# One load moved back in SyncE's queue, and a decoding list started three steps later

## The chip, the cores and the metric

One core of a Trainium2 chip runs the kernel. The metric is device time in microseconds (us), the median of the runs.

## The reference

Three layers in a row. First a linear attention over 2 x 8 heads, 768 positions and 48 channels, with a decay per channel and a bonus for the current position. Its output is read as 1536 tokens of 384 channels. Then a mixture of eight experts:

```python
expert_idx = np.argmax(x @ w_gate, axis=1)
# token i goes to row counts[e] of its expert e while counts[e] < capacity
h = np.maximum(np.einsum('ecd,edf->ecf', disp, w1), 0.0)
y = np.einsum('ecf,efd->ecd', h, w2)
out[i] = gate_w[i] * y[expert_idx[i], pos[i]]
```

with 1024 hidden channels for each expert. Last a gated MLP, `(sigmoid(x @ w_gate) * (x @ w_val)) @ w_out`, with 1536 hidden channels. All in float32.

## The kernel before, in words

Everything is written for one core in an order given by hand; each engine carries out its instructions in that order, and only waits for the data and the buffers of each.

The attention stage ends with the router: it ranks the tokens of each expert, and twelve indirect DMAs from GpSimd (`scatter`, L221) write the scaled tokens to a table in DRAM, `xs_d`, with a stretch of rows for each expert. Expert zero's tokens are also gathered on TensorE, so that its work can begin before the last scatters land.

The expert stage is one loop (L940) of 64 steps, eight for each expert, step i = 8e + f, and three more that finish. A step holds:

- `s1(e, f)` (L891): nine matmuls of 224 columns, the first product for 128 hidden channels. Numbers are split in a high and a low float32r part, hence three matmuls for each of three slices. The relu goes out of PSUM through ScalarE (L903, high part) and VectorE (L904, low part). There are three PSUM buffers `ph`.
- `s2` of step i - 3 (L910): six matmuls, the second product. In steps 7 to 9 and at the experts' borders a list shifts some of them.
- `etr(e, b)` (L876): the transposes of one half b of an expert's rows on TensorE (L883), then `xh` by ScalarE (L886) and `xl` by VectorE (L887). Both halves use the one PSUM tile `xp`. Expert one's two halves stand in step 7, each ahead of one `s2`; for later experts they are in steps f = 4 and f = 6 of the expert before.
- `eload(e)` (L872): the load of an expert's rows from `xs_d`, on SyncE's queue. It waits for all twelve scatters. Expert e + 2's is in step f = 5 of expert e; expert one's stands ahead of the loop (L936).
- `bg` (L135): it converts one expert weight block, a 384 KB tile `raw`, to its high part `rh` on ScalarE (L144) and its low part `rl` on VectorE (L146). Ahead of that it calls `fetch` (L128), which issues the loads of blocks up to five ahead on SyncE. Blocks 0 to 4 are converted in the attention stage; step i converts block 5 + i and, from step 1 on, issues the load of block 9 + i. (Block n is called raw n for short.) Block n uses the buffer of block n - 5 (`NRAW` = 5), so its load waits for the conversion of that one. Blocks 2k and 2k + 1 hold the first and second weights of steps 2k and 2k + 1.
- `tick` (L206): it takes the next operation of a list, `dops`. The list holds the decoding of five blocks of the MLP's weights, 768 KB each as 64-bit numbers: a load on SyncE (`dfetch`, L156, two buffers) and seven operations: one on ScalarE (L166), four on VectorE (L169, L172, L176, L180), the high part on ScalarE (L186) and the low part on GpSimd (L190). Five loads and 35 operations make 40 entries. The first two entries are loads. `tick(2)` ahead of the loop takes them; after that one entry goes with each step from step `T0` to 39, and two with each from step 40.

So SyncE's queue ahead of the loop is: blocks 5 to 9, expert one's rows, two MLP blocks; then blocks 10 to 13 (steps 1 to 4), expert two's rows (step 5), block 14, and so on.

After the expert stage the MLP stage runs 48 steps of matmuls (L1001, L1026) and scatters the output.

Of the kernel before, what the change touches and what calls it, by code (L numbers as in the profile page):

```python
# [21 lines left out]
AHEAD = 5  # L22
OVL = 6
FIRST = 5
T0 = 6
TK = 1
RS = {(5, 1): (0, 1), (6, 0): (2, 3, 4, 5)}
R4E = "ssvsvs"
# [21 lines left out]
NT = 2  # L50
TAILF = 2
EB0 = 7
S20 = {7: (4, 5), 8: (6,), 9: (7,), 10: ()}
EB = (4, 6)
DMAX = (122880.0 - 2.0 ** -7) * 2.0 ** 16
# [54 lines left out]
def body(tc, A, out):  # L110
    nc = tc.nc
    E = mybir.EngineType
    with ExitStack() as top, tc.manual_schedule():
# [14 lines left out]
        def fetch(n):  # L128
            while nxt[0] < n:
                m = nxt[0]  # L130
                nxt[0] += 1
                raw[m] = rpl[0].tile([128, 768], F32, tag="raw", name="raw", bufs=rpl[1])
                nc.sync.dma_start(out=raw[m], in_=A["wx"][m // 2][:, (m % 2) * 768:(m % 2) * 768 + 768])

        def bg(count=1, pool=False, ahead=3, later=None):  # L135
            for _ in range(count):
                n = nxt[1]
                if n == 64:
                    return
                nxt[1] += 1  # L140
                fetch(min(n + ahead, rpl[2]))
                t = raw.pop(n)
                h = rh[n % NR]
                nc.scalar.copy(out=h, in_=t)  # L144
                if later is None:
                    (nc.gpsimd if pool else nc.vector).tensor_sub(rl[n % NR], t, h.bitcast(F32))  # L146
                else:
                    later.append(lambda l=rl[n % NR], t=t, h=h: nc.vector.tensor_sub(l, t, h.bitcast(F32)))
# [57 lines left out]
        def tick(count=1, keep=False):  # L206
            last = None
            for _ in range(count):
                if dops:
                    n, k, f = dops.pop(0)  # L210
                    if keep and (k == 5 and last == n or k == 6 and kept):
                        kept.append(f)
                    else:
                        f()
                    if k == 4:
                        last = n
# [12 lines left out]
        def after(load, done):  # L229
            for i in done:  # L230
                tc.add_manual_dep(load.ins, i.name,
                                  mybir.DependencyInfo(mybir.DependencyClass.Sync, mybir.DependencyReason.DATA),
                                  reason="rows of every scatter")
# [541 lines left out]
        with ExitStack() as ctx:  # L775
# [7 lines left out]
            def c1():  # L783
                ct = pm.tile([128, 8], F32, tag="xp", name="ct", bufs=1)
                nc.tensor.matmul(ct, ones, cnts[:, 0, :], start=True, stop=False)
                nc.tensor.matmul(ct, ones, cnts[:, 1, :], start=False, stop=True)
                nc.vector.tensor_copy(out=cf, in_=ct)
                nc.vector.memset(off[:, 0:1], 0.0)
                for e in range(7):
                    nc.vector.tensor_add(off[:, e + 1:e + 2], off[:, e:e + 1], cf[:, e:e + 1])  # L790
                nc.vector.tensor_copy(out=offi, in_=off[0:1, :])
                nc.vector.reduce_max(out=mxi, in_=cf[0:1, :], axis=AX.X)
# [67 lines left out]
            def c2(b):  # L860
                x, m2, oh, rank, pi, gk = R[b][0:6]
                t = rt.tile([128, 6, 8], F32, tag="tm", name="tm2")
                nc.vector.tensor_mul(t, oh, off.unsqueeze(1).to_broadcast([128, 6, 8]))
                s = rt.tile([128, 6], F32, tag="se", name="se2")
                nc.vector.reduce_sum(out=s, in_=t, axis=AX.X)
                nc.vector.tensor_add(cpos[:, 6 * b:6 * b + 6], s, rank)

            def c3(e):
                offv[e] = nc.values_load(offi[0:1, e:e + 1], engines=[E.DVE, E.Activation], min_val=0, max_val=1536,
                                         skip_runtime_bounds_check_because="expert counts sum to the number of tokens")  # L870

            def eload(e, eng=nc.sync):  # L872
                xr[e] = mp.tile([128, 2, 384], F32, tag="xr", name="xr")
                after(eng.dma_start(out=xr[e][0:NP], in_=xs_d[e * 1536:e * 1536 + NB, :].rearrange("(b p) d -> p b d", p=NP)), scx)

            def etr(e, b):  # L876
                r = xr[e]
                if b == 0:
                    xt[e] = (mp.tile([128, 3, NB], F32R, tag="xh", name="xh", bufs=1),
                             mp.tile([128, 3, NB], F32R, tag="xl", name="xl", bufs=1)) if e % 2 else (xeh, xel)  # L880
                xp = pm.tile([128, 3, NP], F32, tag="xp", name="xp", bufs=1)
                for kt in range(3):
                    nc.tensor.transpose(xp[:, kt, :], r[0:NP, b, kt * 128:(kt + 1) * 128], ident[0:NP, 0:NP])  # L883
                q = slice(b * NP, b * NP + NP)
                xh, xl = xt[e]
                nc.scalar.copy(out=xh[:, :, q], in_=xp)  # L886
                nc.vector.tensor_sub(xl[:, :, q], xp, xh[:, :, q].bitcast(F32))  # L887
# [3 lines left out]
            def s1(e, f):  # L891
                n = 8 * e + 2 * (f // 2)
                wh, wl = rh[n % NR], rl[n % NR]
                xh, xl = xt[e]
                ph = pm.tile([128, NB], F32, tag="ph", name="ph", bufs=3)
                mm = [(kt, a, b) for kt in range(3) for a, b in ((wh, xh), (wh, xl), (wl, xh))]
                if e == f == 0:
                    mm = mm[0::3] + mm[2::3] + mm[1::3]
                for i, (kt, a, b) in enumerate(mm):
                    w = slice(((f % 2) * 3 + kt) * 128, ((f % 2) * 3 + kt) * 128 + 128)  # L900
                    nc.tensor.matmul(ph, a[:, w], b[:, kt, :], start=(i == 0), stop=(i == 8))  # L901
                h = hp.tile([128, 2, NB], F32R, tag="hh", name="hh")
                nc.scalar.activation(out=h[:, 0, :], in_=ph, func=AF.Relu)  # L903
                nc.vector.scalar_tensor_tensor(out=h[:, 1, :], in0=ph, scalar=0.0, in1=h[:, 0, :].bitcast(F32), op0=ALU.max,  # L904
                                               op1=ALU.subtract)
                hs[(e, f)] = h
# [26 lines left out]
            xt[0] = (xeh, xel)  # L933
            plan(PRE)
            fetch(sum(BG) + FIRST)
            eload(1)  # L936
            tick(2)
            seq = [(e, f) for e in range(8) for f in range(8)]
            LAG = 3
            for i in range(64 + LAG):  # L940
                if i == OVP:
                    overflow()
                if i < 64:
                    e, f = seq[i]
                    s1(e, f)
                    if i == 3:
                        c2(0)
                        c2(1)
                    if i == 1:
                        c1()  # L950
                    if i == OVL:
                        offv["most"] = nc.values_load(mxi[0:1, 0:1], min_val=0, max_val=1536,
                                                      skip_runtime_bounds_check_because="at most every token")
                    if f == 3 and e:
                        c3(e)
                    if f in EB and 0 < e < 7:
                        etr(e + 1, EB.index(f))
                    if f == 5 and e < 6:
                        eload(e + 2)
                if i >= LAG:  # L960
                    e, f = seq[i - LAG]
                    if i < 66 - TAILF:
                        for g in (() if f == 0 and e else (0, 1) if f == 1 and e else S20.get(i, (f,))):
                            if i == EB0:
                                etr(1, g - S20[i][0])
                            s2(e, g)
                        if (f == 7 if i > max(S20) else i == max(S20) - 1):
                            for m in range(3):
                                yev(e, m)
                    elif i == 66:  # L970
                        for m in range(3):
                            for g in range(7 - TAILF, 8):
                                s2(7, g, (m,))
                            yev(7, m)
                            xsplit(0, m)
                if sum(BG) - 5 <= i <= 58 and i != OVP - 1:
                    bg(2 if i == OVP else 1, False, AHEAD)
                if i < 64:
                    tick(0 if i < T0 or OVP - NT <= i < OVP else TK if i < 40 else 2)
            tick(len(dops))  # L980
# [97 lines left out]
```

## Time and profile before

| | us |
|---|---|
| median of 3 runs | 463.74 |
| lowest and highest | 463.63, 464.53 |
| the profiled execution | 464.22 |
| its span | 462.5 |
| TensorE busy (PE) | 441.7 (96%) |
| weight loads (PEld) | 415.8 (90%) |
| VectorE (DVE) | 281.8 (61%) |
| ScalarE (ACT) | 218.2 (47%) |
| GpSimd (POOL) | 111.2 (24%) |

The profile is of one execution. The span is from its first to its last instruction; 1.7 us of the execution's own time lie around it. Busy time is that of each engine's instructions; SyncE only issues DMAs. The expert stage lies between 84.4 us and 225 us, the MLP stage after it. PEclk is the clock that TensorE was granted, as a share of 2.4 GHz; 0.5 is the level of 1.2 GHz.

### The profile page before, as it was taken

How to read it: one execution, taken by the hardware profiler on the slowest of the kernel's cores; microseconds unless marked ns; L12 is line 12 of the kernel's file. 1: busy time of each engine (PE TensorE's matmuls, PEld its weight loads, DVE VectorE, ACT ScalarE, POOL GpSimd, SP SyncE). 2: the span in 40 equal slices, each digit the busy share in tenths (PEclk: the TensorE clock that was granted, in tenths of full speed). 3: DMA queues.
4: the chain of work that ended last, by engine and by line, in shares of the span. 5: the costliest groups of instructions: out<-in, count | busy, mean ns of one | idle time of the engine just before them, and what ended most of it. 6: DMA issues, size and time to landing. Idle time of an engine off the chain costs nothing.

```text
span 462.5 us, 8319 instructions
## 1 busy us (share of the span) xinstructions
PE 441.7 (96%) x3227; PEld 415.8 (90%) x3230; DVE 281.8 (61%) x502; ACT 218.2 (47%) x469; POOL 111.2 (24%) x105
## 2 busy tenths in 40 slices
PE   8999999956999999999999999999999999999994
PEld 4688887946999999999889999999999999999993
DVE  6867876736999999775477878777442222222211
ACT  3377778505777776674444343444343222212222
POOL 2555475700202112000033544313113000000013
PEclk9999999996999999999999999999999999999999
DMA  7999904676789876773024353422002000000002
GB/s 242 338 300 320 373 19 141 236 270 217 225 257 302 273 229 203 221 219 142 0 69 122 85 135 71 136 85 54 2 17 87 0 1 1 0 1 0 1 10 92
DMA packets 23194, 63.53 MB, mean 137 GB/s; under 512 B 4592, under 2 KB 8304, under 8 KB 23152
## 3 DMA queue, kind: packets, MB, share of 16 engines
q1 hardware_dynamic: 21088, 58.24, 40.7%
q0 software_dynamic: 1920, 4.73, 2.8%
q8 instruction: 26, 0.43, 0.4%
q14 instruction: 16, 0.13, 0.1%
q10 hardware_dynamic: 144, 0.00, 0.0%
HBM read 55.48 MB, written 7.48 MB: 136 GB/s over the span
## 4 chain that ended last, share of the span: by engine, by line
PE 45%; DVE 3%; issue 2%; ACT 1%; POOL 1%; POOLq 0%; DVEq 0%; ACTq 0%
PE po L1026 15%; PE pv L1001 14%; PE pg L1001 14%; PE ph L901 1%; PE py L920 1%; POOL out_dram L221 1%; DVE wa L176 1%; DVE wa L169 1%; DVE gl L1013 1%; DVE sg L1011 0%; PE py L919 0%; ACT wa L166 0%; ACT x0h L930 0%; DVE wa L172 0%; ACT wy L186 0%
## 5 line engine op out<-in xcount | busy, mean ns | idle before, releaser
L1011 DVE TENSOR_TENSOR sg<-sg,pv 128x384 f32<-128x384 f32 (+2 forms) x49 | 26.6, 543 | 80.5 <-PE pv L1001 79.6
L146 DVE TENSOR_TENSOR rl<-raw,rh 128x768 fp32r<-128x768 f32 x59 | 60.4, 1024 | 19.7 <-ACT rh L144 19.3
L144 ACT CAST rh<-raw 128x768 fp32r<-128x768 f32 x64 | 53.1, 833 | 24.6 <-DMA raw<-in_wx_dram 12.0
L920 PE MATMUL py<-hh,rh 128*128 128x448 f32 x192 | 64.3, 377 | 0.0
L1012 ACT CAST gh<-sg 128x384 fp32r<-128x384 f32 (+2 forms) x49 | 24.8, 506 | 81.9 <-DVE sg L1011 80.5
L190 POOL TENSOR_TENSOR wy<-wa,wy 128x768 fp32r<-128x768 f32 x10 | 20.2, 2023 | 146.5 <-ACT wy L186 116.1
L1013 DVE TENSOR_TENSOR gl<-sg,gh 128x384 fp32r<-128x384 f32 (+2 forms) x49 | 35.8, 730 | 29.4 <-ACT gh L1012 27.9
L919 PE MATMUL py<-hh,rl 128*128 128x224 f32 x192 | 53.1, 276 | 0.0
L1007 ACT ACTIVATE sg<-pg 128x384 f32<-128x384 f32 x48 | 23.5, 490 | 56.9 <-PE pg L1001 56.0
L221 POOL DMA_INDIRECT out_dram<-ob,ids x12 | 11.7, 974 | 119.5 <-ACT ob L1033 117.0
L920 PEld LDWEIGHTS py<-hh,rh 128*128 128x128 f32 x192 | 36.8, 192 | 2.0
L919 PEld LDWEIGHTS py<-hh,rl 128*128 128x128 f32 x192 | 37.3, 194 | 0.0
L1026 PE MATMUL po<-wy,gh 128*128 128x384 f32 x144 | 36.7, 335 | 0.0
L903 ACT ACTIVATE hh<-ph 128x224 fp32r<-128x224 f32 x64 | 22.9, 357 | 24.7 <-PE ph L901 23.5
L372 ACT ACTIVATE at<-cst,dl 128x128 f32<-128x128 f32 x84 | 26.1, 391 | 10.1 <-DVE dl L358 10.1
L904 DVE SCALAR_TENSOR_TENSOR hh<-ph,hh 128x224 fp32r<-128x224 f32 x64 | 24.6, 384 | 10.0 <-ACT hh L903 9.0
L901 PE MATMUL ph<-xh,rh 128*128 128x224 f32 x96 | 26.6, 277 | 0.3 <-PEq L795 0.3
L901 PE MATMUL ph<-xh,rl 128*128 128x224 f32 x96 | 26.8, 280 | 0.0
L901 PE MATMUL ph<-xl,rh 128*128 128x224 f32 x96 | 26.7, 278 | 0.0
L901 PE MATMUL ph<-xeh,rh 128*128 128x224 f32 x96 | 26.2, 275 | 0.0
L901 PE MATMUL ph<-xeh,rl 128*128 128x224 f32 x96 | 26.1, 275 | 0.0
L1026 PEld LDWEIGHTS po<-wy,gh 128*128 128x128 f32 x144 | 26.0, 188 | 0.0
(208 smaller groups left out, 1195.4 us busy)
## 6 DMA issues: line engine op xcount, KB each, us to landing
raw<-in_wx_dram SPq DMA_DIRECT2D x64, 384.0 KB, 5.2
r<-in_wy_dram SPq DMA_DIRECT2D x18, 768.0 KB, 5.8
dm<-in_dm_dram SPq DMA_DIRECT2D x8, 672.0 KB, 11.6
kt<-in_kr_dram SPq DMA_DIRECT2D x8, 576.0 KB, 11.3
xs_d<-zero SPq DMA_DIRECT2D x8, 336.0 KB, 10.0
xr<-xs_d SPq DMA_DIRECT2D x8, 336.0 KB, 7.0
v<-in_v_dram SPq DMA_DIRECT2D x8, 288.0 KB, 8.9
cat<-in_cax_dram SPq DMA_DIRECT2D x1, 404.0 KB
```

The costliest lines, as they stand in the source:

```text
L144: nc.scalar.copy(out=h, in_=t)
L146: (nc.gpsimd if pool else nc.vector).tensor_sub(rl[n % NR], t, h.bitcast(F32))
L372: nc.scalar.mul(AT[s][:, j, :], ident, DL[s][:, j:j + 1])
L901: nc.tensor.matmul(ph, a[:, w], b[:, kt, :], start=(i == 0), stop=(i == 8))
L904: nc.vector.scalar_tensor_tensor(out=h[:, 1, :], in0=ph, scalar=0.0, in1=h[:, 0, :].bitcast(F32), op0=ALU.max, op1=ALU.subtract)
L919: nc.tensor.matmul(y[:, 0, :], wl[:, w], h[:, 0, :], start=(f == 0), stop=False, skip_group_check=True)
L920: nc.tensor.matmul(y, wh[:, w], h, start=False, stop=(f == 7), skip_group_check=True)
L1001: nc.tensor.matmul(pg[g], w[a][:, q], x[b][:, kt, :], start=(kt == 0 and (a, b) == (0, 0)), stop=(kt == 2 and b == 1))
L1011: nc.vector.tensor_mul(gg[:, a:b], sg[:, a:b], pg[1][:, a:b])
L1012: nc.scalar.copy(out=gh[:, a:b], in_=gg[:, a:b])
L1013: nc.vector.tensor_sub(gl[:, a:b], gg[:, a:b], gh[:, a:b].bitcast(F32))
L1026: nc.tensor.matmul(po[i], g[v][:, a], w[u][:, q], start=(f == 0 and (u, v) == (0, 0)), stop=(f == 11 and v == 1))
```

## The change

The load of expert one's rows moves from ahead of the loop to the end of step 3, behind that step's `bg`, and one `tick` goes with it instead of two ahead of the loop. `T0` goes from 6 to 9.

```diff
-T0 = 6
+T0 = 9
...
+LOAD1 = 3
...
             fetch(sum(BG) + FIRST)
-            eload(1)
-            tick(2)
             seq = [(e, f) for e in range(8) for f in range(8)]
...
                     bg(2 if i == OVP else 1, False, AHEAD)
+                if i == LOAD1:
+                    eload(1)
+                    tick()
                 if i < 64:
                     tick(0 if i < T0 or OVP - NT <= i < OVP else TK if i < 40 else 2)
```

SyncE's queue is then: blocks 5 to 9; blocks 10, 11 and 12 (steps 1 to 3); expert one's rows and one MLP block; block 13 (step 4); expert two's rows and block 14 (step 5); and so on. The second MLP block's load goes with step 9, the first decoding operation with step 10, and the list ends in step 43 instead of 41.

## Rows read from the trace of the kernel before

**Rows 1.** Stretches: window, length, busy and count per engine, PEclk, DMA share, GB/s.

```profile
88.00:92.00 4.00, 4.00 (x33) 3.91 (x33) 3.64 (x16) 2.59 (x6) 3.39 (x3) 1.00 0.32 111
92.00:96.00 4.00, 4.00 (x34) 3.92 (x33) 3.86 (x12) 1.19 (x2) 0.08 (x1) 1.00 0.33 99
96.00:100.00 4.00, 2.36 (x18) 1.86 (x16) 0.14 (x1) 0.00 (x0) 0.00 (x0) 1.00 0.91 307
100.00:104.00 4.00, 0.00 (x0) 0.00 (x0) 0.00 (x0) 0.00 (x0) 0.00 (x0) 0.79 0.96 366
...
108.00:112.00 4.00, 3.86 (x16) 3.73 (x17) 2.02 (x4) 1.17 (x2) 0.00 (x0) 0.50 0.66 204
...
140.00:160.00 20.00, 20.00 (x158) 19.57 (x157) 18.91 (x30) 15.15 (x29) 3.25 (x2) 1.00 0.90 277
```

**Rows 2.** Waits of the span: engine, line, waited for, us in total, times, longest.

```profile
ACT rh L144 <- DMA raw<-in_wx_dram: 12.0, 3, 10.9
...
PE xp L883 <- DVE xl L887: 9.4, 1, 9.4
```

**Rows 3.** Timeline of TensorE, 94 to 118 us: start, us, instruction, idle before.

```profile
95.74 0.26 PE L901 MATMUL ph<-xeh,rh 128*128 128x224 f32 x1
...
97.28 0.51 PE L883 MATMUL xp<-cst,xr 112*128 112x112 f32 x3 [0.38 <-DMA xr<-xs_d]
...
98.37 0.38 PE L920 MATMUL py<-hh,rh 128*128 128x448 f32 x1
108.14 0.82 PE L883 MATMUL xp<-cst,xr 112*128 112x112 f32 x3 [9.39 <-DVE xl L887]
...
110.54 0.39 PE L901 MATMUL ph<-xh,rh 128*128 128x224 f32 x1
...
112.43 0.36 PE L919 MATMUL py<-hh,rl 128*128 128x224 f32 x1
```

**Rows 4.** Timeline of VectorE, 94 to 124 us.

```profile
95.76 0.38 DVE L904 SCALAR_TENSOR_TENSOR hh<-ph,hh 128x224 fp32r<-128x224 f32 x1
105.15 0.96 DVE L146 TENSOR_TENSOR rl<-raw,rh 128x768 fp32r<-128x768 f32 x1 [9.01 <-ACT rh L144]
...
107.57 0.51 DVE L887 TENSOR_TENSOR xl<-xp,xh 128x336 fp32r<-128x336 f32 x1
109.47 0.51 DVE L887 TENSOR_TENSOR xl<-xp,xh 128x336 fp32r<-128x336 f32 x1 [1.38 <-ACT xh L886]
```

**Rows 5.** Timeline of ScalarE, 94 to 124 us.

```profile
104.28 0.83 ACT L144 CAST rh<-raw 128x768 fp32r<-128x768 f32 x1 [10.88 <-DMA raw<-in_wx_dram]
```

**Rows 6.** Timeline of SyncE's queue, 50 to 145 us.

```profile
94.01 0.33 SPq L874 DMA_DIRECT2D xr<-xs_d  x1
94.93 0.81 SPq L158 DMA_DIRECT2D r<-in_wy_dram  x2
95.85 3.23 SPq L133 DMA_DIRECT2D raw<-in_wx_dram  x4
99.13 0.43 SPq L874 DMA_DIRECT2D xr<-xs_d  x1
```

**Rows 7.** Timeline of GpSimd, 66 to 94 us, the last scatter.

```profile
90.50 1.58 POOL L221 DMA_INDIRECT xs_d<-xs,pi  x1 [0.30 <-DVE mxi L792]
```

**Rows 8.** Timeline of VectorE, 66 to 94 us, the low parts of blocks 5 and 7.

```profile
87.09 0.96 DVE L146 TENSOR_TENSOR rl<-raw,rh 128x768 fp32r<-128x768 f32 x1 [0.33 <-issue]
...
91.44 0.95 DVE L146 TENSOR_TENSOR rl<-raw,rh 128x768 fp32r<-128x768 f32 x1
```

**Rows 9.** Views of lines L133 (weight blocks) and L874 (experts' rows): landing times.

```profile
DMA to landing us min/median/max: 3.1/5.2/14.4
...
DMA to landing us min/median/max: 7.0/7.6/8.2
```

**Rows 10.** Timeline of VectorE, 168 to 196 us.

```profile
180.19 0.96 DVE L180 SCALAR_TENSOR_TENSOR wa<-r,wa 128x768 int32<-128x768 int32 x1
181.07 0.39 DVE L904 SCALAR_TENSOR_TENSOR hh<-ph,hh 128x224 fp32r<-128x224 f32 x1
```

## The prediction, on record before the change was run

> **What bounds the kernel now.** I read the span in stretches first, then the waits, then each engine's timeline around the one hole, then SyncE's queue. The stretches [rows 1] show TensorE busy for all of 88 to 96 us and again from 112 us on (20.00 of 20.00 us in 140 to 160), while 96 to 100 holds 2.36 us of work and 100 to 104 none. The clock is granted in full at first; the share for 100 to 104 is 0.79 and for 108 to 112 it is 0.50, so TensorE, idle since 98.7, falls to the 1.2 GHz level and restarts there.
>
> The waits name the hole [rows 2]: one wait of 9.4 us of a transpose of expert one's rows (L883) for VectorE's xl, and on ScalarE a longest wait of 10.9 us for a weight load. The timelines join them. TensorE [rows 3] does the first half's transposes of expert one (97.28, step 7), six matmuls of step 4's second product up to 98.4, and then the second half's transposes only at 108.14, because both halves share one PSUM tile, which VectorE must empty. VectorE [rows 4] has nothing to do from 95.76 + 0.38 to 105.15, then two subtractions and two relu halves, and only then xl at 107.57. The first subtraction waits for ScalarE's conversion of weight block raw 10, which started at 104.28 after 10.88 us of idling for that load [rows 5]. So one late load, at the head of two in-order engines, holds TensorE, which does not need that block before step 10.
>
> Why it is late stands in SyncE's queue [rows 6]: the load of expert one's rows goes out at 94.01, two 768 KB loads of MLP blocks from 94.93, and raw 10 to 13 only from 95.85. The first of them waited for the scatters, the last of which GpSimd issued from 90.50 to 92.08 [rows 7]. Raw 10 itself needs just the buffer of raw 5, which VectorE was done with at 87.09 + 0.96 = 88.05 [rows 8]. In 88 to 92 the DMA share was 0.32 [rows 1]: there was room.
>
> **The change, part by part.** *The load moves behind raw 10, 11 and 12.* These three no longer wait for the scatters. Raw 10 goes out at about 88.1 instead of 95.85, and raw 12 when raw 7's subtraction ends, 91.44 + 0.95 = 92.4 [rows 8]; raw 11 lies between, about 91.3. A raw load lands 3.1 to 14.4 us after issue, median 5.2 [rows 9]; with nothing but one another and the scatters ahead I take the median. Raw 10 is then there at 93.3, before ScalarE and VectorE come to it. Raw 11 lands at about 96.5 and its conversion ends 0.83 later [rows 5], at 97.3, just when VectorE wants it (below): no slack, and every microsecond more is paid in full. The bounds are no cost (3.1 us) and 9.2 us (14.4 us).
>
> *The load of expert one's rows itself* still waits for the scatters, so it goes out at 94.01 at the earliest. Now it lands after 97.28 - 94.01 = 3.27 us [rows 3, 6]; the other loads of this line need 7.0 to 8.2 us [rows 9], each behind an MLP block and a weight block just issued. Here raw 11 and 12 went out 2.7 and 1.6 us before it; 384 KB take 1.1 us at the 366 GB/s of 100 to 104 [rows 1], so little is left of them. I take 0.4 us over today: rows at 97.7, bounds 97.3 and 102.6 (8.2 us after 94.4).
>
> The DMA page of the Trainium skill (DMA: Bandwidth & Descriptors, section Queues, rings and completion order) has a rule against this: each DMA engine takes its queue rows in turn, packet by packet, so raw 11 and 12 would halve the pace of the last scatters, which now run alone. No run here shows it yet; by that rule the rows would come some 0.7 us later than today, and the time would be about 0.3 us above my sum.
>
> *The chain to the end of step 8's first product.* VectorE: after the relu half of 95.76 the next subtraction can start at about 96.1; from there to xl it needs what it needs now, 107.57 - 105.15 = 2.42 us [rows 4], so xl ends at 96.1 + 2.42 + 0.51 = 99.0. TensorE: from transposes to the end of xl the second half takes 109.47 + 0.51 - 108.14 = 1.84 us, with transposes of 0.82 us at the 1.2 GHz level; at 2.4 GHz they take 0.51 [rows 3], so 1.53. Rows at 97.7 give xl at 99.2, the later of the two. The second half follows 0.06 us on, its xl ends at 100.8, and step 4's and 5's second products run beside this. Step 8's nine matmuls need that xl from the second one on; at 0.12 us each (33 or 34 in 4 us, [rows 1]) they end at 101.8. Now they run from 110.54 to 112.43, at half the clock [rows 3]. The gain is 112.43 - 101.8 = **10.6 us**, the clock included. Were TensorE to wait for nothing after the rows arrive at 97.3, step 8 would end at about 97.3 + 2 x 0.3 (transposes) + 12 x 0.16 + 1.06 = 100.9: 11.5 us is the most.
>
> *What is late next.* Raw 13 goes out behind the rows (336 KB) and now one MLP block instead of two, at about 95.4. Raw 10, behind both, took from 95.85 to 104.28 at most, 8.4 us [rows 5, 6]; so raw 13 lands by 103.8. Behind it on ScalarE stands the relu of step 9; TensorE first misses that when step 12 wants its PSUM buffer, about 106.6, which leaves raw 13 until 105.0. I cost it at nothing. Expert two's rows follow raw 13 and are wanted at step 12 as well.
>
> *Decoding from step nine.* The second MLP block's load moves to step 9's tick, and ScalarE's first decoding op from step 6 to step 10. Of the 40 operations in the list, one goes behind the moved load, 31 in steps 9 to 39, and 8 in steps 40 to 43 at two a step; now it is 34 in steps 6 to 39 and the last 4 in steps 40 and 41. No operation is added. What it takes out of steps 6 to 9 also leaves ScalarE free in front of xh: with the start kept at step 6 that operation would wait there for the MLP block. In the end four more double ticks lie on VectorE. Today the last two decoding operations of step 40 end at 180.19 + 0.96, and step 41's relu half starts at 181.07 [rows 10], ends at 181.46, and is wanted when step 44 reuses its buffer, about 182.2: 0.7 us to spare. After the change the two fall in step 42, with step 40 free of them, so I take nothing, with bounds of 0 and 1.9 us (both operations uncovered).
>
> *The rest.* From step 9 to the end TensorE is busy throughout [rows 1], with the same work, so the gain should reach the end undiminished. **Sum:** the profiled execution took 464.22 us (span 462.5 and 1.7 around it), 464.22 - 10.6 = 453.6. The median of the runs is 463.74, 0.48 lower, so on that footing 453.1.
>
> **The rivals.** *A, the loads come late* (chance 0.14): the rows land as the six others of this line did, 7.6 us after issue, at 102.0, or raw 11 does. TensorE then idles for over 5 us and falls to 1.2 GHz as now, which costs about 2 us of restart (half of 108.14 to 112.43): gain 10.6 - 4.3 - 2 = 4.3, time 459.4; half as late and without the clock, 455.2. For it: six of seven loads of this line are that slow. Against: what stands ahead of them.
>
> *B, VectorE becomes the bound* (0.10): decoding now meets each expert's transposes (xl, twice 0.5 us) instead of its output additions, and the end is denser. Price 1 to 3 us, 454.1 to 456.1. For it: 0.7 us of slack today. Against: no long wait of TensorE for VectorE appears after 112 us, and VectorE starts with four operations fewer.
>
> *C, no change* (0.02): the load order doesn't matter because the DMA engines limit, the hole just moving to raw 13: 463.7. Against: the share of 0.32 in 88 to 92.
>
> *D, slower* (0.03): the wait moves to the rows. The first half's transposes stand in front of everything on TensorE, where the late weight block of today stood behind six matmuls. If the rows land later than 97.7 + 10.6 - 2, about 106.3 (the clock then falls too), the time passes today's; at the 14.4 us of the longest raw load, from 94.4, they land at 108.8: some 2.5 us above, 466.2. Against: 12 us are half as much again as the worst landing of this kind.
>
> **How the numbers follow.** My forecast (gain 10 to 11.5, 452.2 to 453.8) has 0.71, the likeliest single value being 453.1. The range reaches down to the most that the chain can give, 463.74 - 11.5 = 452.2, and up to 455.6, which takes in most of B and the milder half of A; about 0.13 stays outside. A measurement here tells about 0.2 per cent, 0.93 us, from no change. Faster: forecast, A and B, 0.95; same 0.02; slower 0.03.
>
> **What would show it.** In the profile after: raw loads on SyncE at about 88, 91 and 92, before the rows at 94 to 95; ScalarE's 10.9 us wait gone; the second transposes of expert one near 99 instead of 108.14; the clock at full from 96 to 116; TensorE's work from step 9 on unchanged and about 10.6 us earlier. Wrong would be a wait of over 1 us for the rows (A, D), new waits of L901 or L883 for VectorE near steps 40 to 46 (B), or ScalarE waiting for raw 13 beyond step 12 (C).

## The result, and the profile of the changed kernel

The changed kernel takes 455.82 us (median of 4 runs, 455.30 to 456.54) against 463.84 us of the kernel before beside it (4 runs, 463.63 to 464.53): a ratio of 0.9826, 95% interval 0.9806 to 0.9845. It is 8.0 us faster, and the forecast was 10.6 us and 453.1 us; 455.8 lies 0.2 us above the range. The profiled execution took 456.54 us, its span 454.8. All lines of the code have moved down by one (L883 is L884, L919 is L920).

One thing is needed for the runs that follow: in some executions of several kernels the attention stage ends about 1 to 5 us later (step 0 begins at 85 to 90 us instead of 84), in code that no kernel here changes; so I read times before step 9 only in profiles in which step 0 begins near 84 us, and name the others.

TensorE's timeline of the changed kernel, 98 to 112 us, answers to [rows 3]: the transposes of expert one's two halves, the matmul that follows step 8's first product, and expert two's transposes.

```profile
99.28 0.51 PE L884 MATMUL xp<-cst,xr 112*128 112x112 f32 x3 [2.40 <-DMA xr<-xs_d]
...
100.86 0.74 PE L884 MATMUL xp<-cst,xr 112*128 112x112 f32 x3
...
104.76 0.28 PE L920 MATMUL py<-hh,rl 128*128 128x224 f32 x1
...
110.67 0.46 PE L884 MATMUL xp<-cst,xr 112*128 112x112 f32 x3
```

The 9.4 us wait for `xl` is gone and the second transposes stand at 100.86 instead of 108.14. In its place stands a wait of 2.40 us for the rows themselves. Step 8's first product ends at 104.76, where it ended at 112.43 before: 7.67 us, and the spans differ by 7.7 us, so all that was won by then reached the end. The forecast had that point at 101.8.

SyncE's queue, which answers to [rows 6]:

```profile
78.35 14.37 SPq L134 DMA_DIRECT2D raw<-in_wx_dram  x8
95.76 0.33 SPq L875 DMA_DIRECT2D xr<-xs_d  x1
96.15 0.45 SPq L159 DMA_DIRECT2D r<-in_wy_dram  x1
96.70 0.37 SPq L134 DMA_DIRECT2D raw<-in_wx_dram  x1
```

The eight weight loads (raw 5 to 12) are all out by 92.4 to 92.7, as forecast, and ScalarE no longer waits for one. But the rows leave at 95.76 instead of 94.01, though GpSimd issues the last scatter at the same time as before:

```profile
90.47 1.58 POOL L222 DMA_INDIRECT xs_d<-xs,pi  x1 [0.30 <-DVE mxi L793]
```

VectorE's timeline, 94 to 104 us, answers to [rows 4]:

```profile
98.07 0.38 DVE L905 SCALAR_TENSOR_TENSOR hh<-ph,hh 128x224 fp32r<-128x224 f32 x1
100.30 0.51 DVE L888 TENSOR_TENSOR xl<-xp,xh 128x336 fp32r<-128x336 f32 x1 [1.85 <-ACT xh L887]
102.11 0.51 DVE L888 TENSOR_TENSOR xl<-xp,xh 128x336 fp32r<-128x336 f32 x1 [1.30 <-ACT xh L887]
```

VectorE is ready at 98.45 and idles for the rows: the engine that was the cause is not late any more. The stretches (the columns of [rows 1]) show what the wait costs:

```profile
96.00:100.00 4.00, 1.60 (x14) 1.41 (x14) 2.45 (x5) 1.29 (x3) 0.00 (x0) 1.00 0.82 268
100.00:104.00 4.00, 3.89 (x18) 3.46 (x17) 1.97 (x3) 1.43 (x3) 0.00 (x0) 0.62 1.03 336
104.00:108.00 4.00, 4.00 (x31) 3.92 (x30) 2.03 (x4) 2.15 (x6) 0.00 (x0) 0.95 0.67 259
```

In 100 to 104 TensorE is busy for 3.89 us but ends 18 instructions where 33 go in 4 us of full clock: the granted clock is 0.62 on average there. Behind the idle 2.40 us TensorE went down to 1.2 GHz once more: read microsecond by microsecond, the clock is 0.50 from 101 to 104 and 1.00 again from 105.

The DMA engines show what holds the rows. One microsecond, 89 to 90 us, of the kernel before (first) and of the changed one (second), queue by queue: packets, MB, share of 16 engines. Queue q0 carries the scatters, q1 what SyncE issues.

```profile
q0 software_dynamic: 44, 0.18, 50.5%
```

```profile
q1 hardware_dynamic: 34, 0.10, 90.1%
```

Before, 44 packets of the scatters move 0.18 MB. After, raw 10 begins here: 34 packets of 3 KB hold 90.1% of the engines (14.4 engine-us over 34 packets, 0.42 us each; in 84 to 85 us of the kernel before, where weight loads move alone, 152 packets of 2.7 KB hold 103.0% for the same time, 0.11 us each), and not one packet of a scatter moves. Much the same comes again in 92 to 93 us, as raw 11 begins.

```profile
q1 hardware_dynamic: 20, 0.06, 88.1%
q0 software_dynamic: 10, 0.02, 6.1%
```

### The profile page after: what moved, and what is told of

It reads as the page before. It is cut to its first block, busy times and chain, and to the rows that moved or that the text cites. A ratio compares the mean times of both kernels' runs of the same rounds, so it can differ in the third digit from the quotient of the medians.

```text
span 454.8 us, 8312 instructions
## 1 busy us (share of the span) xinstructions
PE 440.9 (97%) x3227; PEld 415.3 (91%) x3230; DVE 282.0 (62%) x502; ACT 218.1 (48%) x469; POOL 109.9 (24%) x105
## 4 chain that ended last, share of the span: by engine, by line
PE 46%; DVE 3%; issue 2%; ACT 1%; POOL 1%; POOLq 0%; DVEq 0%; ACTq 0%
PE po L1028 15%; PE pv L1003 15%; PE pg L1003 15%; PE ph L902 1%; PE py L921 1%; POOL out_dram L222 1%; DVE wa L177 1%; DVE wa L170 1%; DVE gl L1015 1%; DVE sg L1013 0%; PE py L920 0%; ACT wa L167 0%; ACT x0h L931 0%; DVE wa L173 0%; ACT wy L187 0%
## 5 line engine op out<-in xcount | busy, mean ns | idle before, releaser
L920 PE MATMUL py<-hh,rl 128*128 128x224 f32 x192 | 53.0, 276 | 0.0
L191 POOL TENSOR_TENSOR wy<-wa,wy 128x768 fp32r<-128x768 f32 x10 | 18.7, 1872 | 140.3 <-ACT wy L187 140.3
L920 PEld LDWEIGHTS py<-hh,rl 128*128 128x128 f32 x192 | 37.2, 194 | 0.0
L373 ACT ACTIVATE at<-cst,dl 128x128 f32<-128x128 f32 x84 | 26.1, 392 | 10.6 <-DVE dl L359 10.6
L902 PE MATMUL ph<-xh,rl 128*128 128x224 f32 x96 | 26.7, 278 | 0.0
L902 PE MATMUL ph<-xh,rh 128*128 128x224 f32 x96 | 26.4, 275 | 0.3 <-PEq L796 0.3
L902 PE MATMUL ph<-xl,rh 128*128 128x224 f32 x96 | 26.6, 277 | 0.0
L902 PE MATMUL ph<-xeh,rh 128*128 128x224 f32 x96 | 26.2, 275 | 0.0
L902 PE MATMUL ph<-xeh,rl 128*128 128x224 f32 x96 | 26.1, 275 | 0.0
```

The lines of the kernel that those rows point to most:

```text
L373: nc.scalar.mul(AT[s][:, j, :], ident, DL[s][:, j:j + 1])
L920: nc.tensor.matmul(y[:, 0, :], wl[:, w], h[:, 0, :], start=(f == 0), stop=False, skip_group_check=True)
```

## The experiments

Two theories on the late rows. **S**: the weight loads take from the scatters by their bytes, so fewer bytes ahead bring the rows back to 94. **P**: each weight load that starts beside the scatters holds them 1 to 1.5 us, whatever its size. A third, **T**, says that the start of the decoding and not the load's place decides the time. Kernels of one paragraph ran on one chip.

**The two parts alone, half the bytes, the products first.** The first of these keeps `T0` = 6 and moves the load, the second does the reverse:

```diff
-T0 = 9
+T0 = 6
```

> The moved load alone; decoding starts at step 6 again (its second MLP block goes out with step 6, its first operation comes with step 7). Theory S (the last scatters share the DMA engines with raw 10 to 12, so expert one's rows leave and land about 2 us later than before, and TensorE's clock falls): the start of decoding is not what was won or lost; rows again leave at about 95.7 and land near 99.3, time 455.3 to 456.6, as with the whole change. Rival D (the later start of decoding carries a part of the gain, since its first operation stood ahead of xh on ScalarE): 457 or more, with a new wait of ScalarE or VectorE in 100 to 110 us.

> Decoding from step 9 alone; the load of the rows and the two MLP blocks stay ahead of the loop. Theory S: the late raw 10 stays, TensorE still waits some 9.4 us for xl, time 463.0 to 464.5. Rival D: faster than 462.5.

The load alone: 459.25 us (456.18 to 462.57, 7 runs), 0.9913 [0.9874, 0.9952]. The later decoding alone: 465.10 us (8 runs), 1.0032 [1.0016, 1.0048]. T falls: the load carries the gain. But the profile of the first (456.18 us, span 454.4) holds a second lesson. Its rows leave at 95.31 and its clock stays up, so step 8's first product ends at 102.82, 1.94 us ahead of the changed kernel, and its span is only 0.4 us shorter. What it loses again lies far behind. The stretch of 160 to 180 us of this kernel, and its one long wait there:

```profile
160.00:180.00 20.00, 19.25 (x152) 18.62 (x151) 18.35 (x31) 14.11 (x27) 5.71 (x3) 1.00 0.64 191
```

```profile
PE py L920 <- DVE x L926: 0.7, 1, 0.7
```

The changed kernel works 20.00 us in the same stretch and has no such wait; here TensorE waits 0.7 us for an addition of an expert's output on VectorE (L926). From expert two's first transposes to the end this kernel needs 345.67 us; the changed kernel needs 454.8 - 110.67 = 344.13, the kernel before 462.5 - 118.43 = 344.07. The other half of the change needs 345.85, and in its 180 to 200 us TensorE works 18.62 of 20 us, with a wait of 1.38 us for VectorE ahead of an expert's transposes (190.43). The first decoding operation stands in step 6 before, in 7 in the first of these kernels, in 9 in the second, in 10 in the changed one. So it seems to matter where the list's operations fall on the eight steps of an expert: of the four starts, 7 and 9 cost 1.5 to 1.8 us more than 6 and 10. That it is this phase is argued from four kernels, not varied further, and the two waits shown are half of the loss in the first and most of it in the second.

The third loads only the first half of raw 10 to 12; it leaves the second half out, and the conversions read the first half twice (that part of the edit isn't shown):

```diff
+HALF = (10, 11, 12)
...
-                nc.sync.dma_start(out=raw[m], in_=A["wx"][m // 2][:, (m % 2) * 768:(m % 2) * 768 + 768])
+                c = 384 if m in HALF else 768
+                nc.sync.dma_start(out=raw[m][:, 0:c], in_=A["wx"][m // 2][:, (m % 2) * 768:(m % 2) * 768 + c])
...
```

> The changed kernel, but raw 10 to 12 load only half of their bytes (192 KB each; the conversions read that half twice, so the weights of these three blocks are not the reference's and the engines' work is the same). Theory S: half the competing bytes, so about half of the 1.75 us go: rows leave at 94.6 to 95.1, land near 98.2, the clock falls for a shorter time or not at all, time 453.9 to 455.2. Rival Q (the rows leave late for a reason that has nothing to do with the bytes ahead, such as their place in SyncE's queue or a late write receipt): rows leave at 95.6 to 95.9, time 455.3 to 456.6.

It took 455.03 us (453.58 to 459.27), 0.9826 [0.9761, 0.9892], but in its profile step 0 begins at 86.1 us and raw 12's place in the queue holds the rows, not the scatters (rows out at 96.41). It tells nothing on S and P, and was run again below. The fourth changes step 7: the second products of steps 4 to 7 there, the halves of the transposes behind the second and third of them.

```diff
-S20 = {7: (4, 5), 8: (6,), 9: (7,), 10: ()}
+S20 = {7: (4, 5, 6, 7), 8: (), 9: (), 10: ()}
...
-                            if i == EB0:
-                                etr(1, g - S20[i][0])
                             s2(e, g)
+                            if i == EB0 and g in (5, 6):
+                                etr(1, g - 5)
```

> The changed kernel, but in step 7 the second products of steps 4 and 5 stand ahead of the first transposes of expert one's rows, that of step 6 between the halves and that of step 7 behind the second half (they were in steps 7, 7, 8 and 9). Theory S (the miss is TensorE idling for late rows, then running at 1.2 GHz): twelve matmuls fill 1.9 of the 2.4 us, the clock stays at 2.4 GHz or falls for under 1 us, the gap left is 0.5 to 1 us at the rows and 0.2 to 0.5 at step 8; time 452.2 to 453.5. Rival (the conversions on VectorE, not the rows, set step 8's start): 454.5 or more, with TensorE waiting for xl.

458.41 us (452.95 to 458.96, 4 runs), 0.9849 [0.9785, 0.9913]. The profile has step 0 at 89.43 us, so it shows only that the products cover the wait for the rows (0.20 us left of it) when these come late; inconclusive as to time.

**The changed kernel again; the rows first; raw 12 behind the rows.** The last of these ran with step 7 as it is, and with the products first.

```diff
             fetch(sum(BG) + FIRST)
+            eload(1)
...
-                    eload(1)
                     tick()
```

```diff
-LOAD1 = 3
+LOAD1 = 2
```

> The changed kernel once more, for comparison on this chip. Theory S (the last scatters share the DMA engines with raw 10 to 12): where step 0 starts at about 84.4 us the rows leave near 95.7 and land near 99.3, time 455.3 to 456.6. Where the attention stage ends late by x us, the rows are held by raw 12, which waits for step 2's conversion, and the time is longer by up to x, since no stall is left to swallow x: up to 460 for x of 5. Rival (the spread has nothing to do with the end of the attention stage): spans counted from step 0 differ by more than 1.5 us.

> Expert one's rows stay ahead of the loop as before the change, so they wait for the scatters in front of raw 10; only the two MLP blocks move (the first to step 3, the second to step 9). Theory S: rows leave at 94.0 and land at 97.3, raw 10 leaves at 94.4 and lands at 98 to 99 instead of 104.3, so most of the gain comes without moving the rows; TensorE's second transposes at 102 to 103, idle for some 4 us, clock falls, time 455.5 to 457.5. Rival (raw 10 has to leave before the scatters are through for any of the gain): 460 or more.

> The load of the rows one step earlier, behind raw 10 and 11 alone; raw 12 follows the rows and the first MLP block. Theory S: less traffic beside the last scatters, rows leave at 94.3 to 95.2 and land at 97.8 to 98.6, raw 12 still in time for step 7's conversion; 0.5 to 1.5 us faster than the changed kernel in the same call. Rival Q (the rows' lateness does not depend on raw 12's bytes): within 0.4 us of the changed kernel, or slower because raw 12 comes late.

> As the last one, and in step 7 the second products of steps 4 and 5 ahead of the first transposes, those of steps 6 and 7 behind the first and the second half. Theory S: TensorE has work through the wait, the clock stays at 2.4 GHz in 96 to 108 us, 2 to 4 us faster than the changed kernel in the same call, 452 to 453.5 where step 0 starts at 84.4 us. Rival (VectorE's conversions set step 8's start): within 1 us of the changed kernel.

The changed kernel: 457.77 us (454.64 to 460.70, 5 runs), 0.9852 [0.9790, 0.9914]. In its profile step 0 begins at 89.62 us, and from expert two's transposes to the end it needs 458.0 - 113.81 = 344.19 us, no more than before: what is longer lies ahead of them. With the rows ahead of raw 10 and only the MLP blocks moved: 459.25 us (7 runs), 0.9876 [0.9835, 0.9917]. Its rows leave at 93.99, with the scatters as undisturbed as before, but raw 10 to 12 only go out from 94.82, and the old wait is back at half its length:

```profile
103.22 0.82 PE L884 MATMUL xp<-cst,xr 112*128 112x112 f32 x3 [4.51 <-DVE xl L888]
```

So taking two 768 KB loads from ahead of raw 10 is worth about half of the gain (4.1 of the 7.7 us by which the spans differ), and the load's place the rest. With `LOAD1` = 2: 457.48 us (456.66 to 459.53), 0.9880 [0.9836, 0.9924], and with the products first 456.36 us (453.58 to 458.52), 0.9844 [0.9790, 0.9899]; neither can be told from the changed kernel. The profile of `LOAD1` = 2 has step 0 at 84.28, and its rows leave at 96.01 though raw 12 isn't ahead of them: raw 12's bytes don't hold them. That leaves raw 10 and 11, which both start among the scatters. The line below shows the wait for the rows, 2.60 us, and transposes that take 0.82 us, as at the low clock of [rows 3], not 0.51.

```profile
99.37 0.82 PE L884 MATMUL xp<-cst,xr 112*128 112x112 f32 x3 [2.60 <-DMA xr<-xs_d]
```

**The rows behind raw 10 alone; half the bytes again; two loads each.** The first moves `eload(1)` to step 1 and leaves the tick; the third splits each of raw 10 and 11 into two DMAs.

```diff
+                if i == 1:
+                    eload(1)
                 if i == LOAD1:
-                    eload(1)
                     tick()
```

```diff
-                nc.sync.dma_start(out=raw[m], ...
+                for c in ((0, 384), (384, 768)) if m in (10, 11) else ((0, 768),):
+                    nc.sync.dma_start(out=raw[m][:, c[0]:c[1]], ...
```

> Load of expert one's rows right behind raw 10 alone, at step 1 of the expert loop; raw 11 and 12 go out after it, the tick of the MLP's decoding stays where the change has it. Theory P (each weight load that starts beside the scatters holds their packets for 1 to 1.5 us, whatever its size): one start instead of two lies ahead of the rows, so they go out about 0.8 to 1.2 us earlier than in the changed kernel, at 94.5 to 95.0 us where step 0 starts at 84.3, and the clock stays up, since TensorE's wait falls under 2 us. Theory S (the scatters and the loads share by bytes): 768 of 1152 KB less ahead, rows at 94.4 to 94.7. Both expect an earlier load; the rival to both, that only the loop's own pace sets it, expects 95.7 again. Raw 11 loaded later must still be there for step 4: if not, a wait of ScalarE for raw shows at step 3 or 4 and takes the gain back. Time 453.5 to 456.

> The kernel with half the bytes in raw 10 to 12 once more (their conversions read the half twice, so the weights of these blocks are not the reference's), for a profile in which step 0 starts at 84.3 us and the scatters, not raw 12's place in the queue, hold the rows. Theory P: the loads start at the same moments, so the rows still leave at 95.3 to 96.0. Theory S: half the bytes take half the share, so the rows leave at 94.5 to 95.0. If step 0 starts late again, the rows are held by raw 12 and the profile tells the two apart only by the scatters' packets while raw 10 starts.

> Raw 10 and raw 11 each loaded by two DMAs of 192 KB instead of one of 384 KB: the same bytes, twice the starts. Theory P in its strict form (a price for each start): two more starts ahead of the rows, so they leave 1 to 2.5 us later than in the changed kernel, at 96.8 to 98.2 us where step 0 starts at 84.3; in a weaker form (a price for each moment at which loads start beside the scatters) they leave at 95.5 to 96.0, as does theory S, by bytes. Time 455.5 to 458.

All three profiles have step 0 at 83.9 to 84.3 us. One fence for each kernel: the rows on SyncE's queue.

```profile
94.03 0.33 SPq L875 DMA_DIRECT2D xr<-xs_d  x1
```

```profile
93.88 0.33 SPq L883 DMA_DIRECT2D xr<-xs_d  x1
```

```profile
95.52 0.33 SPq L876 DMA_DIRECT2D xr<-xs_d  x1
```

One whole load ahead (384 KB) makes the scatters 0.2 us later, two halves of 192 KB 0.35 us, four of 192 KB as much as two of 384 (the table below has the differences). The rows of the first two are earlier than either theory had them. P, a price for each start, falls; S fits in a form that neither expectation had: some 384 KB cost the scatters next to nothing, and what exceeds them delays them. With four loads of half the size the scatters' packets do move in every microsecond (25 of them in 90 to 91 us beside 47 of the weights, where the changed kernel has 13 beside 96), and the rows are no earlier for it. So the microsecond without a scatter's packet goes with the large packets and isn't what makes the rows late.

The kernel with half the bytes is the test of the whole forecast, since it has the rows at the time that I assumed: 453.64 us (452.82 to 454.03, 4 runs), 0.9783 [0.9740, 0.9827]. TensorE waits 0.86 us for the rows, the clock is 1.00 throughout, the second transposes stand at 98.86, and the matmul behind step 8's first product at 101.43:

```profile
97.28 0.51 PE L892 MATMUL xp<-cst,xr 112*128 112x112 f32 x3 [0.86 <-DMA xr<-xs_d]
...
98.86 0.51 PE L892 MATMUL xp<-cst,xr 112*128 112x112 f32 x3
...
101.43 0.27 PE L928 MATMUL py<-hh,rl 128*128 128x224 f32 x1
```

The kernel with raw 10 alone ahead took 457.02 us, 0.9859 [0.9817, 0.9902], slower than the 453.5 to 456 expected: its rows are there, and raw 11, issued at 94.88, is not. ScalarE's, VectorE's and TensorE's timelines give the chain:

```profile
98.67 0.83 ACT L145 CAST rh<-raw 128x768 fp32r<-128x768 f32 x1 [3.50 <-DMA raw<-in_wx_dram]
```

```profile
99.54 0.96 DVE L147 TENSOR_TENSOR rl<-raw,rh 128x768 fp32r<-128x768 f32 x1 [2.39 <-ACT rh L145]
```

```profile
101.27 0.51 PE L884 MATMUL xp<-cst,xr 112*128 112x112 f32 x3 [2.42 <-DVE xl L888]
```

It is the chain of the kernel before, shortened from 9.4 to 2.42 us, and the clock fell behind it as well. The two-loads kernel came to 455.88 us, 0.9824 [0.9772, 0.9875], as the changed one.

**Half of raw 11, and raw 11's lateness covered.** Three kernels: rows behind raw 10 with the products first; raw 10 and the first half of raw 11 ahead; the same with the products first.

```diff
+                for c in ((0, 384), (384, 768)) if m == 11 else ((0, 768),):
...
+                    if m == 11 and c[0] == 0:
+                        cb[0](1)
...
+            cb[0] = eload
...
-                    eload(1)
                     tick()
```

> Rows right behind raw 10, raw 11 and 12 behind the rows, and in step 7 the second products of steps 4 to 7 ahead of and between the two halves of the transposes. The kernel with the rows behind raw 10 alone had them out at 94.03 us, but its raw 11 landed late: ScalarE waited 3.5 us for it, VectorE 2.39 us after that, and TensorE 2.42 us ahead of the second half of the transposes. If that chain is what took its gain back, four products of about 1 us each ahead of the transposes cover it: no wait of TensorE over 1 us between 92 and 108 us, clock at 1.00 there, and 453 to 455 us. If something later takes it back (the decoding's phase), the span from 108 us on is longer by as much and the time stays at 456 to 457.

> Raw 10 and the first half of raw 11 (192 KB) ahead of the rows, the second half behind them: 576 KB instead of 384 (rows out at 94.03 us) or 768 KB (95.5 to 96.0 us) beside the scatters. Theory S with a slack (the DMA engines have room for some bytes beside the scatters, and what exceeds it delays the scatters' completion): rows out between 94.0 and 95.0 us. Theory P (the second start itself delays them): 95.3 us or later. Raw 11's second half then lands near 97 us, so ScalarE waits for it about 1 us where the changed kernel did not; time 454 to 456.5.

> The same with the second products of steps 4 to 7 ahead of and between the halves of the transposes: the rows as early, and up to 2 us of TensorE's work over the waits for the rows and for raw 11's second half. If these two waits and the clock that they cost are the whole miss, the time is that of the forecast, 452.5 to 454; if the decoding's later waits set it, 455 to 457.

In that order: 454.94 us, 0.9826 [0.9791, 0.9860]; 455.58 us, 0.9832 [0.9795, 0.9869]; 453.76 us (452.61 to 455.16), 0.9802 [0.9762, 0.9842]. The products first don't cover all of raw 11's lateness: waits of 1.69 and 1.48 us are left ahead of the second transposes in the first and the third, where I had expected none over 1 us in the first, though the clock stays at 1.00. With 576 KB ahead the rows leave at 94.86 and 94.79: between the two ends, as S with some room says. The forecast's time seemed to be back in a kernel that leaves nothing out, so the last pair put it beside the changed kernel on one chip:

> The changed kernel again, on the same chip and beside the next run: 455.3 to 457.8 us, and in a profile whose step 0 starts at 84 us the rows out at 95.3 to 96.0 us again.

> The kernel with raw 10 and half of raw 11 ahead of the rows and the products of step 7 first, again, beside the changed kernel. If the late rows and the clock that falls behind them are most of the miss, it stays 1.5 to 2.5 us under the changed kernel on the same chip, at 453 to 455 us; if its 453.76 us came from the chip alone, the two medians are within 0.8 us.

The changed kernel 454.68 us (454.46 to 454.89, 5 runs), 0.9801 [0.9786, 0.9817]; the other 454.94 us (454.07 to 456.09, 5 runs), 0.9805 [0.9783, 0.9827]. They can't be told apart, and the gain of the changed kernel is 9.6 us on this chip, a little more than I had expected. Its profile shows why: step 0 begins 0.46 us earlier (83.93), the rows were nearly as late (95.09), TensorE waited 2.04 us, and this time the clock didn't fall.

```profile
98.46 0.51 PE L884 MATMUL xp<-cst,xr 112*128 112x112 f32 x3 [2.04 <-DMA xr<-xs_d]
...
100.04 0.51 PE L884 MATMUL xp<-cst,xr 112*128 112x112 f32 x3
...
102.61 0.27 PE L920 MATMUL py<-hh,rl 128*128 128x224 f32 x1
```

```profile
100.00:104.00 4.00, 3.95 (x29) 3.61 (x29) 1.93 (x4) 2.25 (x4) 0.00 (x0) 1.00 1.04 318
```

From the landing to the end of step 8's first product it is 102.61 - 98.46 = 4.15 us here and 104.76 - 99.28 = 5.48 us in the first profile: the same program at the two levels, so the fall of the clock costs 1.33 us. The idle 2.04 us here left the clock at 1.00, and 2.06 us in the kernel with two loads each brought it down to 0.50. That as good as the same idle time once costs the clock and once not fits what the Trainium skill says (TensorE: Matmul & The Clock Gate, section What's actually happening): the hardware looks at the activity on a schedule of its own, which doesn't begin with the program. No run here shows that schedule. The other kernel reaches expert two's transposes at 108.38, 0.14 us earlier than this one, and needs 344.82 us from there instead of 344.18: in 116 to 118 us TensorE works 1.64 of 2 us, with a wait of 0.36 us for VectorE's low part of expert two's rows (117.33), where this one works 2.00. What it wins it gives back. No version that loads all of its bytes was clearly faster than the changed kernel.

Side by side, from the profiles with step 0 at 83.9 to 84.4 us (us; the wait is that of the rows or of the second transposes, the longer):

| kernel | KB of raw 10 and 11 ahead, begun beside the scatters | rows out, less last scatter's issue | longest wait | clock fell | expert two's transposes | from there to the end |
|---|---|---|---|---|---|---|
| before | 0 | 94.01 - 90.50 = 3.51 | 9.39 | yes | 118.43 | 344.07 |
| rows first | 0 | 93.99 - 90.48 = 3.51 | 4.51 | yes | 114.26 | 344.14 |
| raw 10 ahead | 384 | 94.03 - 90.32 = 3.71 | 2.42 | yes | 111.36 | 344.24 |
| half bytes | 384 | 93.88 - 90.02 = 3.86 | 0.86 | no | 107.34 | 344.66 |
| half of raw 11 | 576 | 94.86 - 90.23 = 4.63 | 1.57 | yes | 110.91 | 344.19 |
| load alone | 768 | 95.31 - 90.43 = 4.88 | 1.83 | no | 108.73 | 345.67 |
| changed, last | 768 | 95.09 - 90.03 = 5.06 | 2.04 | no | 108.52 | 344.18 |
| two loads each | 768 | 95.52 - 90.27 = 5.25 | 2.06 | yes | 109.77 | 344.13 |
| changed, first | 768 | 95.76 - 90.47 = 5.29 | 2.40 | yes | 110.67 | 344.13 |
| `LOAD1` = 2 | 768 | 96.01 - 90.36 = 5.65 | 2.60 | yes | 110.51 | 344.39 |

The second column leaves raw 12 out. It goes out ahead of the rows too, at about 92 us, in the kernels with half bytes (192 KB), the load alone, the change, and two loads each (384 KB). `LOAD1` = 2, without it, has the latest rows, so it isn't what holds them. But with it the kernel with half bytes has 576 KB ahead, as many as half of raw 11, and its rows are 0.77 us earlier: that the delay goes by bytes rests on raw 12 coming too late to count. Raw 11 alone, begun beside the scatters without raw 10, was not run either, so whether the sum of the bytes or raw 11's late start sets the delay is not shown.

## Why the prediction was off

The range was missed by little: its end, 455.6, lies inside the measured interval (454.8 to 456.7 us), and on the last pair's chip the same kernel took 454.68, inside the range, with rows nearly as late. On which side of 455.6 the time falls hangs on whether the clock falls, and no figure here foretells that; the first step below was wrong in either case.

**What bounded the kernel: right.** One late weight load held ScalarE, VectorE and TensorE in turn; with that load early the 10.88 us, the 9.01 us and the 9.39 us [rows 3 to 5] are gone together, and a kernel with raw 11 late again (raw 10 ahead) brings all three back in small.

**Raw 10 to 12: right.** They went out by 92.4 to 92.7 and no conversion waited for them; raw 11's began at 95.92, before VectorE wanted it. VectorE's time for the first `xl`, 99.0, had it free from 98.45, in time for that: right as well.

**The step that failed** is "The load of expert one's rows itself still waits for the scatters, so it goes out at 94.01 at the earliest", from which the sum took 97.7 for the landing. The scatters' own end moved: with raw 10 and 11 started among them they were done 1.75 us later, though issued at the same time. The landing took 99.28 - 95.76 = 3.52 us, against the 3.27 + 0.4 of the sum. So the rows were there at 99.28 and not at 97.7: 1.6 us. A wait of over 1 us for the rows was named ahead as a sign of being wrong; 2.40 us came. The DMA share of 0.32 that I read as room [rows 1] was room for one load, not for two: with raw 10 alone ahead the scatters end 0.2 to 0.4 us later, and with raw 11 too another 1.0 to 1.9. My bounds held the value (97.3 to 102.6), the point didn't.

The sentence beside that step on the Trainium skill (DMA: Bandwidth & Descriptors, section Queues, rings and completion order: an engine takes its rows in turn, packet by packet) had the direction right and less than half the size, 0.7 us for a measured 1.75. It named raw 11 and 12; the runs show raw 11 behind raw 10, and that raw 12 doesn't matter (`LOAD1` = 2). That both move in turn is what the kernel with two loads each shows (25 packets beside 47); in the changed kernel no scatter packet moves in 89 to 90 us, which the rule as I used it doesn't give.

**The second step that failed is that the clock was taken as kept** once the rows arrive. The wait of 2.40 us cost the clock, and 1.33 us with it; in the other profile, at 2.04 us, it didn't. Together: 1.6 + 1.3 = 2.9 of the 104.76 - 101.8 = 3.0 us that are missing at the end of step 8's first product. Rival A had this pair, the late rows and the clock behind them, at 0.14, with the rows either 4.3 or some 2 us late; its milder half, 455.2, left the clock out, and the range, which was to take it in, ended at 455.6.

**The chain behind the rows: right.** With half the bytes, the rows as early as I had put them, everything else follows: TensorE at 101.43 where 101.8 was forecast, and 453.64 us where 453.1 was.

**Decoding from step nine: right in the sum, in part by luck.** It costs 344.13 - 344.07 = 0.06 us, less than the 0.1 us to which a span is given, and rival B's price doesn't appear (20.00 of 20.00 us in 160 to 180 and in 180 to 200, no wait of L902 or L884 for VectorE near steps 40 to 46). But kept at six it would have cost 1.5 us, and one step earlier (first operation in step 9, with the loads as before) it cost 1.8: I had costed only how late the last operations are, not where on an expert's steps they all fall.

**Raw 13, C and D: right.** Nothing waits for raw 13; no rival of "slower" came.

What stays open: why step 0 begins late in some executions (in the three profiles with step 0 at 88.8 to 89.6 us TensorE idles 1.7 to 2.1 us in 72 to 76 us of the attention stage and its clock falls to 0.50 behind that; in the two with 85.0 and 86.1 it stays at 1.00), and what about the second 384 KB makes the scatters late, its bytes or its start.

## What to carry to other kernels

A load that waits for earlier transfers isn't only moved in its queue: whatever now goes out ahead of it shares the DMA engines with the very transfers that it waits for, so their end must be costed anew. Put behind the waiting load what isn't due yet, but only that: with raw 11 behind the rows its conversion began 2.8 us later (98.67 against 95.92 us), and TensorE's wait for that, 2.42 us, was as long as the one for the late rows. And where a wait of about 2 us of TensorE is left over, cost it with and without the fall of the clock, since the same program does both.

## What the runs showed of the hardware

- Weight loads that start beside indirect scatters: packets of 3 KB took 0.42 us each (34 of them, 90.1% of 16 engines for 1 us) where those of weight loads alone took 0.11 (152 of 2.7 KB in 84 to 85 us of the kernel before), and the scatters stood still in that microsecond; loads of half the packet size ran beside the scatters without a stop and ended no sooner.
- With 384 KB of raw 10 and 11 begun beside the scatters the rows waited 0.2 to 0.4 us longer (the most in the kernel with raw 10 ahead and the products first, 94.12 - 90.19 = 3.93), with 576 KB 1.1, with 768 KB 1.4 to 2.1 (from the table, less 3.51; raw 12 left out as there).
- TensorE's granted clock stayed at 1.00 after idle times of 1.69 (raw 10 ahead, products first), 1.83 and 2.04 us and fell to 0.50 after 2.06, 2.40, 2.42 and 2.60 us; it fell too after two shorter ones, 1.44 us up to 98.06 and 1.57 us up to 101.10 (half of raw 11 ahead).
